# Another order of loads and blocks in the opening of a fused window attention and MLP kernel

## The chip, the cores and the metric

The kernel runs on one core of a Trainium2 chip. The metric is the device time of one execution in microseconds; the kernel before has a median of 288.01 us over three runs (287.84 to 289.57).

## The reference

Sliding-window attention, whose output feeds a two-layer MLP with a sigmoid-approximated gelu. Eight sequences of 576 tokens, 8 heads of 64; a token sees the 32 tokens on either side of it in its own sequence.

```python
scores = scale * np.matmul(q, k.transpose(0, 1, 3, 2))
mask = np.abs(pos[:, None] - pos[None, :]) <= 32
scores = np.where(mask, scores, -1000000000.0)
attn = np.exp(scores - max); attn = attn / sum
x = np.matmul(attn, v)                   # 4608 tokens x 512
h = x @ w_in                             # 512 -> 2048
g = h * (1.0 / (1.0 + np.exp(-1.702 * h)))
out = g @ w_out                          # 2048 -> 512, float32
```

## The kernel before, in words

The 4608 tokens are 36 units of 128 keys and 128 queries (the queries shifted by 32), four units to a tile of 512 tokens, nine tiles in all. A unit goes through these steps. `scores` (L238): 24 small matmuls into two PSUM banks (tag "t" is a pair of banks; "A", "C", "B", "E", "LA", "LB" are single ones), then two exponentials on ScalarE (L256) into `p`. `band` (L258): VectorE multiplies `p` by a 0/1 mask (L264). `values` (L266): 16 matmuls with `ve` (v as loaded) and `vo` (v shifted by 64 rows, built by `odd_v`, L201, from this unit's and the next unit's v), a column of ones giving the sums. `norm` (L284): VectorE divides. `x_T` and `x_T2` (L298, L313): TensorE transposes one unit's or two units' x, and VectorE or ScalarE copies it into `xT`.

A tile's layer 1 is `layer1_plain` for tile 0 (L378): sixteen blocks of 8 matmuls, each block followed by a gelu on ScalarE. From tile 1 on it is `l1_group` (L407): four groups of seven products by Strassen's scheme, which need sums of w_in (`w1_sums`, L327, in `a`) and of x (`x_sums`, L349, in `xs`), both made by VectorE. Layer 2 of tile 0 is plain (`layer2_plain`, L464): 64 matmuls of 512 columns, taken one by one from the list `l2` wherever the order has room for them; those of later tiles are Strassen's again (`layer2`, L492). Exponential and gelu need different tables on ScalarE, and each change of kind is a table load.

The order of every engine is written out by hand: an engine takes its instructions in the order in which the program names them and waits at each until its inputs and its buffer are there. Nothing is planned at run time. `opening` (L562) names everything up to the first product of tile 1; `run` (L785) then calls `x_sums(1)` and `first_layer1` (L845), whose four groups take 8 matmuls of `l2` each, and after it the scores of tile 2 and whatever is left in `l2`. All loads of inputs are issued by GpSimd, in the order of the program, so a load stands behind GpSimd's copies and mask work; each load of GpSimd also waits for the eighth load before it. The first 576 keys and queries are loaded in an order of their own (`load_first`, L137: two parts, each over 64 partitions) and transposed by TensorE (`T_first`, L157); the second tile's come with `load_four` and `T_four` (L173, L181). `keep_busy` (L553) issues filler matmuls on a tile of zeros, which TensorE runs while it has nothing else.

In the opening before, units 0 and 1 go through attention first, then the second half of k and q is transposed, four layer 1 blocks run between units 2 and 3, then twelve blocks between the transposes and attention of units 4 to 7, with 24 of the 64 matmuls of `l2`.

## Time and profile before

| | |
|---|---|
| runs | 287.84, 288.01, 289.57 us |
| profiled execution | 289.7 us, span of its instructions 288.0 us |
| TensorE busy | 277.7 us (96%) |
| VectorE, ScalarE, GpSimd busy | 218.3, 193.9, 126.9 us |
| chain that ended last | TensorE 87%, VectorE 4%, ScalarE 3% |
| read from HBM, written | 36.83 MB, 9.44 MB |

A row of the timeline has the start in us from the span's start, the time that the merged instructions took, the engine, the line of the program, the operation, output and inputs, shapes and the count; in brackets the idle time of the engine before it and what ended it. PE is TensorE's matmul, PEld its loading of weights, DVE is VectorE, ACT ScalarE, POOL GpSimd. Rows of helper lines (L67, L70) are told apart by their tiles: `sc` scores, `pv` values, `tp` transposes, `h` layer 1, `o` layer 2, `junk` filler. A row of a transfer has its count, size and the time from issue to landing.

### The profile page before, as it was taken

To read this page: it belongs to the slowest core of one execution; us is meant where nothing else is said; L and a number is where in the kernel's file an instruction comes from. 1 tells how busy PE (TensorE), PEld (TensorE's weight loads), DVE (VectorE), ACT (ScalarE), POOL (GpSimd) and SP (SyncE) were. 2 spreads that over 40 slices of the span, in tenths; PEclk is the share of its full clock that TensorE was granted. 3 is DMA by queue.
4 is the path that set the end of the run, shared out by engine and by line. 5 is a ranking of instruction groups with operands and counts; after the bars stand their busy time and mean duration, and the time that the engine had idled before them with its cause. 6 is when DMAs were issued, how large, how long until landed. Compare 5 with 4: busy or idle time off the path is not lost.

```text
span 288.0 us, 9119 instructions
## 1 busy us (share of the span) xinstructions
PE 277.7 (96%) x3770; PEld 229.8 (80%) x3770; DVE 218.3 (76%) x502; ACT 193.9 (67%) x340; POOL 126.9 (44%) x192
## 2 busy tenths in 40 slices
PE   7997999999999998999999999999999999999994
PEld 5775856777678887888888888888888888888883
DVE  0676798888877986798879887978788878946731
ACT  2437594789887668676967696689668865568410
POOL 8965457599499954467155917350210000000000
PEclk9999999999999999999999999999999999999999
DMA  8999999999999999999979999998432150301033
GB/s 94 188 193 198 184 204 153 177 99 140 184 134 153 209 132 198 93 180 146 182 106 181 142 177 100 193 116 148 95 77 64 47 112 12 81 2 73 2 110 112
DMA packets 146986, 37.37 MB, mean 130 GB/s; under 512 B 133888, under 2 KB 142592, under 8 KB 146944
## 3 DMA queue, kind: packets, MB, share of 16 engines
q0 software_dynamic: 104464, 18.42, 91.4%
q1 hardware_dynamic: 42032, 17.84, 34.8%
q8 instruction: 29, 0.48, 0.7%
q10 hardware_dynamic: 448, 0.52, 0.6%
q14 instruction: 13, 0.11, 0.1%
HBM read 36.83 MB, written 9.44 MB: 161 GB/s over the span
## 4 chain that ended last, share of the span: by engine, by line
PE 87%; DVE 4%; ACT 3%; issue 2%; DMA 2%; ACTq 0%; POOLq 0%
PE h L70 39%; PE o L70 36%; PE pv L70 3%; PE sc L70 3%; DVE x L294 2%; DMA kq<-in_k_dram 2%; PE junk L70 2%; ACT p L256 1%; PE tp L168 1%; PE tp L322 1%; ACT L256 1%; DVE p L264 1%; PE tp L189 1%; PE tp L232 1%; DVE rec L293 1%
## 5 line engine op out<-in xcount | busy, mean ns | idle before, releaser
L419 ACT ACTIVATE g<-h 128x512 f16<-128x512 f32 x128 | 72.1, 598 | 35.9 <-PE h L70 35.7
L70 PEld LDWEIGHTS <-g 128*128 128x128 f16 x576 | 54.5, 98 | 9.7
L70 PEld LDWEIGHTS <-a 128*128 128x128 f16 x512 | 49.3, 98 | 11.0 <-issue 0.8
L70 PE MATMUL h<-xs,a 128*128 128x256 f16 x384 | 57.6, 272 | 0.1
L70 PE MATMUL o<-w,g 128*128 128x256 f16 (+1 forms) x320 | 55.1, 294 | 0.0
L70 PEld LDWEIGHTS <-w 128*128 128x128 f16 x512 | 49.2, 98 | 7.3 <-issue 0.6
L70 PE MATMUL h<-xT,w 128*128 128x256 f16 x384 | 53.9, 273 | 0.6 <-issue 0.5
L199 POOL DMA_DIRECT2D ve<-in_v_dram x40 | 34.3, 863 | 44.0 <-issue 37.0
L70 PEld LDWEIGHTS <-gs 128*128 128x128 f16 x384 | 36.9, 98 | 6.2 <-issue 1.5
L256 ACT ACTIVATE p<-sc 128x512 bf16<-128x512 f32 x72 | 36.6, 619 | 3.7 <-PE sc L70 3.6
L70 PE MATMUL o<-b,gs 128*128 128x256 f16 x256 | 37.8, 273 | 1.3 <-issue 0.9
L70 PE MATMUL o<-b,g 128*128 128x256 f16 x256 | 37.3, 273 | 0.0
L432 DVE TENSOR_TENSOR h<-h,s 128x512 f32<-128x512 f32 x32 | 22.4, 698 | 18.7 <-PE h L70 18.7
L67 ACT COPY h<-h 128x512 f32<-128x512 f32 x32 | 18.7, 585 | 16.5 <-PE h L70 16.1
L131 POOL DMA_DIRECT2D kst<-in_k_dram x31 | 26.4, 855 | 6.9 <-PE tp L232 3.4
L131 POOL DMA_DIRECT2D qst<-in_q_dram x35 | 28.1, 805 | 2.8 <-DMA w<-in_moe_w_out_dram 2.7
L294 DVE TENSOR_TENSOR x<-pv,rec 128x256 f16<-128x256 f32 (+1 forms) x53 | 27.6, 520 | 1.8
L264 DVE TENSOR_TENSOR p<-p,mask 128x1024 bf16<-128x1024 bf16 x36 | 24.7, 687 | 2.6 <-ACT p L256 2.6
L438 DVE TENSOR_TENSOR h<-h,s 128x512 f32<-128x512 f32 x32 | 22.4, 700 | 4.7 <-PE h L70 4.2
L209 POOL COPY vo<-ve 64x264 int32<-64x264 int32 x28 | 13.1, 467 | 25.8 <-PE pv L70 24.7
L67 ACT COPY s<-h 128x512 f32<-128x512 f32 x32 | 19.1, 598 | 1.5 <-PE h L70 0.2
L70 PE MATMUL h<-xs,w 128*128 128x256 f16 x128 | 19.2, 273 | 0.0
(85 smaller groups left out, 367.9 us busy)
## 6 DMA issues: line engine op xcount, KB each, us to landing
out_dram<-o_sb SPq DMA_DIRECT2D x33, 256.0 KB, 3.0
ve<-in_v_dram POOLq DMA_DIRECT2D x32, 128.0 KB, 5.8
kst<-in_k_dram POOLq DMA_DIRECT2D x25, 128.0 KB, 5.9
qst<-in_q_dram POOLq DMA_DIRECT2D x21, 128.0 KB, 5.7
w<-in_moe_w_in_dram POOLq DMA_DIRECT2D x4, 512.0 KB, 8.7
w<-in_moe_w_out_dram POOLq DMA_DIRECT2D x4, 512.0 KB, 13.5
qst<-in_q_dram POOLq DMA_DIRECT2D x7, 96.0 KB, 5.1
kq<-in_q_dram POOLq DMA_DIRECT2D x2, 256.0 KB, 6.2
```

What stands on the lines that cost most here:

```text
L67: (eng.copy if eng is self.nc.scalar else eng.tensor_copy)(out, in_)
L70: self.nc.tensor.matmul(out, lhsT, rhs, start=start, stop=stop, skip_group_check=True)
L131: self.nc.gpsimd.dma_start(t[off:off + n], src[b, :, s:s + n, :].rearrange("h s d -> s h d"))
L168: self.nc.tensor.transpose(tp[64 * (h % 2):64 * (h % 2) + 64, h // 2, x, :], src[:, 4 * i + h, x, :], self.ident[r, r])
L199: self.nc.gpsimd.dma_start(t[off:off + n, :, :self.D], self.v[b, :, s:s + n, :].rearrange("h s d -> s h d"))
L209: eng.tensor_copy(words(vo[64:128]), words(self.ve[u % 9][64:128]))
L256: self.nc.scalar.activation(p[:, eo].rearrange("k h s -> k (h s)"), sc[eo], AF.Exp, scale=self.scale)
L264: (eng or self.nc.vector).tensor_mul(pv, pv, msk.to_broadcast([128, 8, 2, SQ]))
L294: dve.tensor_mul(x[:, 4 * at:4 * (at + n), :].rearrange("p (b h) d -> p b h d", b=n), acc[:, :, :, :D], r.to_broadcast([128, n, 4, D]))
L419: act.activation(g[:, f, 256 * half:256 * half + 256], bank.rearrange("p (i n) -> p i n", i=2), AF.Gelu_apprx_sigmoid)
L432: dve.tensor_add(e, b, s7)
L438: dve.tensor_add(c, b, s7)
```

## The change

- The first halves of k and q come in two loads each, over all 128 partitions, and are transposed with 128 columns instead of 64. v of units 0 to 3 and half of unit 4's are loaded ahead of w_in, the rest of unit 4's behind it; loads of v go ahead of w_out's.
- A matrix `far` (0 inside the window, -8e9 outside) is built by GpSimd. For units 0 to 3 and 5 to 7, TensorE adds it to the scores by two matmuls of 512 columns with the identity ahead of the scores; these units have no `band`. The 0/1 mask for the other units is made from `far` by VectorE, later.
- Units 0 to 3 go through attention ahead of layer 1. The sixteen blocks of tile 0 run in the order of w_in's quarters. The scores of units 4 to 7 are issued together, each in its own pair of banks.
- The opening takes 8 matmuls of `l2`, each group of `first_layer1` 14. All sums of w_in's second half stand at the end of the opening, ahead of `x_sums(1)`. The `odd_v` copies of units 3, 4 and 6 go to GpSimd. Fillers have half the width.

```diff
--- before.py
+++ after.py
@@ -96,19 +97,25 @@
         self.idle = cst.tile([128, 512], BF16, name="idle")
         self.spark = cst.tile([128, 1], F32, name="spark")
 
+    def setup_far(self):
+
+        pool, m = self.nc.gpsimd, self.far
+        lo, hi = slice(0, 64), slice(64, 128)
+        pool.memset(m, 0.0)
+        for b, rows, sign in ((0, lo, 1), (0, hi, -1), (1, lo, -1), (1, hi, 1)):
+            ap = m[rows, b, :]
+            pool.affine_select(out=ap, in_=ap, compare_op=ALU.is_ge, fill=-8.0e9, base=0,
+                               pattern=[[-sign, SQ]], channel_multiplier=sign)
+
     def setup_mask(self):
-        pool, m = self.nc.gpsimd, self.mask
+
+        dve, m = self.nc.vector, self.mask
         lo, hi = slice(0, 64), slice(64, 128)
-        pool.memset(m, 1.0)
-        for blks, rows, sign in ((slice(0, 2), lo, 1), (slice(0, 2), hi, -1), (slice(2, 4), lo, -1), (slice(2, 4), hi, 1)):
-            ap = m[rows, blks, :]
-            pool.affine_select(out=ap, in_=ap, compare_op=ALU.is_ge, fill=0.0, base=0,
-                               pattern=[[0, 2], [-sign, SQ]], channel_multiplier=sign)
-
-    def cut_mask(self):
-        lo, hi = slice(0, 64), slice(64, 128)
+        for b in range(2):
+            dve.tensor_scalar(out=m[:, 2 * b:2 * b + 2, :], in0=self.far[:, b:b + 1, :].to_broadcast([128, 2, SQ]),
+                              scalar1=0.0, scalar2=None, op0=ALU.is_ge)
         for b, rows, cols in ((0, hi, slice(0, 32)), (0, lo, slice(32, 64)), (2, lo, slice(0, 32)), (2, hi, slice(32, 64))):
-            self.nc.gpsimd.memset(self.mask[rows, b, cols], 0.0)
+            dve.memset(m[rows, b, cols], 0.0)
 
     def load_w1(self, c, n=1):
         w = 512 * n
@@ -135,13 +142,21 @@
     FIRST = {"k": ((0, 320, 5), (320, 256, 4)), "q": ((32, 256, 4), (288, 256, 4))}
 
     def load_first(self, c, part):
+
+        D = self.D
         if "first" not in self.stage:
-            s = self.sb("g", [128, self.H, 9, self.D], BF16, 2, "kq1")
-            self.stage["first"] = {"k": s[:, :, 0:5], "q": s[:, :, 5:9]}
+            s = self.sb("g", [128, 68 * D], BF16, 2, "kq1")
+            self.stage["first"] = {("k", 0): s[:, 0:20 * D], ("q", 0): s[:, 20 * D:36 * D],
+                                   ("k", 1): s[0:64, 36 * D:68 * D], ("q", 1): s[64:128, 36 * D:68 * D]}
         lo, n, j = self.FIRST[c][part]
-        src = {"q": self.q, "k": self.k}[c]
-        self.nc.gpsimd.dma_start(self.stage["first"][c][64 * part:64 * part + 64, :, 0:j],
-                                 src[0, :, lo:lo + n, :].rearrange("h (p j) d -> p h j d", j=j))
+        src = {"q": self.q, "k": self.k}[c][0, :, lo:lo + n, :].rearrange("h (p j) d -> p h (j d)", j=j)
+        dst = self.stage["first"][c, part]
+        if part:
+            self.nc.gpsimd.dma_start(dst.rearrange("p (h x) -> p h x", h=8), src)
+            return
+        for g in range(2):
+            self.nc.gpsimd.dma_start(dst[64 * g:64 * g + 64].rearrange("p (h x) -> p h x", h=4),
+                                     src[:, 4 * g:4 * g + 4, :])
 
     def kq_tile(self, t):
 
...
@@ -159,16 +174,24 @@  (T_first, the first half's new form)
+            tp = self.bank(tag, [128, j, 2, 64], BF16, "tp")
+            for x in range(j):
+                for h in range(2):
+                    self.nc.tensor.transpose(tp[64 * h:64 * h + 64, x].rearrange("x g p -> x (g p)"), src[:, 2 * i + h, x, :],
+                                             self.ident)
+            self.copy(eng, dst[:, i:i + 3:2, :].rearrange("x g (p j) -> x g p j", j=j), tp.rearrange("x j g p -> x g p j"))
...
@@ -198,6 +221,13 @@
         for off, b, s, n in self.pieces(128 * u, 128):
             self.nc.gpsimd.dma_start(t[off:off + n, :, :self.D], self.v[b, :, s:s + n, :].rearrange("h s d -> s h d"))
 
+    def load_v_part(self, lo, n):
+        u, at = divmod(lo, 128)
+        t = self.ve[u % 9]
+        for off, b, s, m in self.pieces(lo, n):
+            self.nc.gpsimd.dma_start(t[at + off:at + off + m, :, :self.D],
+                                     self.v[b, :, s:s + m, :].rearrange("h s d -> s h d"))
+
     def odd_v(self, u, eng):
 
         vo = self.vo[u % 5]
@@ -235,7 +265,7 @@
 
 
 
-    def scores(self, u, tag):
+    def scores(self, u, tag, far=False):
         kT, q = self.kT[u], self.qT[u]
         nxt = self.k_first if u == self.NU - 1 else self.kT[u + 1][:, :, 0:64]
         if tag == "t":
@@ -243,13 +273,17 @@
             sc = [sc[:, 0], sc[:, 1]]
         else:
             sc = [self.bank(x, name="sc") for x in tag]
+        if far:
+            m = self.far.rearrange("p (o b) s -> p o b s", o=1).to_broadcast([128, 4, 2, SQ])
+            for eo in range(2):
+                self.mm(sc[eo].rearrange("p (o b s) -> p o b s", b=2, s=SQ), self.ident, m, start=True)
         for hp in range(4):
             c = 128 * hp
             for eo in range(2):
                 r = slice(64 * eo, 64 * eo + 64)
                 lo, hi = sc[eo][0:64], sc[eo][64:128]
-                self.mm(lo[:, c:c + 64], kT[r, hp, 0:64], q[r, hp, 0:64], start=(hp == 0))
-                self.mm(hi[:, c:c + 128], kT[r, hp, 64:128], q[r, hp, :], start=(hp == 0))
+                self.mm(lo[:, c:c + 64], kT[r, hp, 0:64], q[r, hp, 0:64], start=(hp == 0 and not far))
+                self.mm(hi[:, c:c + 128], kT[r, hp, 64:128], q[r, hp, :], start=(hp == 0 and not far))
                 self.mm(lo[:, c + 64:c + 128], nxt[r, hp, :], q[r, hp, 64:128], start=False)
         p = self.p[u] = self.sb("p", [128, 2, 8, SQ], BF16, 4)
         for eo in range(2):
@@ -569,128 +603,109 @@
             dve.memset(t[:, :, self.D:], 1.0)
         self.load_first("k", 0)
         self.load_first("q", 0)
+        self.load_v(0)
         make_identity(nc, self.ident)
         act.activation(self.spark, self.spark, AF.Exp)
-        for u in (0, 1, 2):
-            self.load_v(u)
+        self.load_v(1)
+        self.load_first("k", 1)
+        self.setup_far()
+        self.load_first("q", 1)
+        self.load_v(2)
+        self.load_v(3)
+        self.load_v_part(512, 64)
         self.load_w1(0)
-        self.setup_mask()
-        self.load_first("k", 1)
-        self.load_first("q", 1)
-        self.cut_mask()
         self.load_w1(1)
-        self.load_v(3)
-        self.load_v(4)
+        self.odd_v(3, pool)
         self.load_w1(2)
         self.load_four("k")
         self.load_four("q")
         self.load_w1(3)
+        self.load_v_part(576, 64)
+        for u in (5, 6, 7, 8):
+            self.load_v(u)
+        for c in range(4):
+            self.load_w2(c)
         dve.tensor_copy(self.identh, self.ident)
-        self.keep_busy(20, "E")
+        self.keep_busy(44, "E", 128)
         self.T_first("k", 0, "AC", (dve, act))
-        self.keep_busy(6, "E")
+        self.keep_busy(4, "E", 128)
         self.T_first("q", 0, ("LA", "LB"), (dve, act))
-        self.keep_busy(4, "E")
-        for u in (5, 6):
-            self.load_v(u)
-        self.load_w2(0)
-        for u in (7, 8):
-            self.load_v(u)
-        for c in (1, 2, 3):
-            self.load_w2(c)
-        self.load_kq("k", 8)
-        self.scores(0, "t")
-        self.scores(1, "AC")
+        self.scores(0, "t", True)
+        self.scores(1, "AC", True)
         self.odd_v(0, dve)
+        self.keep_busy(6, "E", 128)
+        self.values(0, "t")
+        self.norm(0)
+        self.T_first("k", 1, ("LA", "LB"), (act, act))
+        self.keep_busy(8, "E", 128)
+        self.T_first("q", 1, "BE", (dve, act))
         self.odd_v(1, dve)
-        self.keep_busy(10, "E")
-        self.band(0)
-        self.band(1)
-        self.values(0, "t")
+        self.odd_v(2, dve)
+        self.keep_busy(10, "t", 128)
+        self.scores(2, "t", True)
+        self.scores(3, ("LA", "LB"), True)
         self.values(1, "AC")
-        self.norm(0)
         self.norm(1)
-        self.keep_busy(6, "E")
-        self.x_T(0, "LA", act)
-        self.keep_busy(4, "E")
-        self.x_T(1, "LB", act)
-        self.T_first("k", 1, "AC", (dve, dve))
-        h, n, gelus = [], [0], []
+        self.keep_busy(4, "B", 128)
+        self.values(2, "t")
+        self.norm(2)
+        self.x_T2(0, "A", act)
+        self.values(3, ("LA", "LB"))
+        self.norm(3)
+        self.x_T(2, "E", act)
+        h, n = ["C", "B", "LA", "LB", "C", "B", "A", "E", "LA", "LB", "B", "E"], [0]
 
         def l1(half, *ds):
             for d in ds:
-                self.layer1_plain(0, d, half, h[n[0] % len(h)])
+                self.layer1_plain(0, d, half, h[n[0]])
                 n[0] += 1
 
-        self.layer1_plain(0, 0, 0, "B", gelus)
-        self.T_first("q", 1, ("LA", "LB"), (dve, act))
-        self.layer1_plain(0, 1, 0, "E", gelus)
-        self.odd_v(2, dve)
-        self.odd_v(3, dve)
-        h[:] = ["LB", "B", "E"]
-        self.scores(2, "t")
-        self.scores(3, "AC")
-        self.layer1_plain(0, 2, 0, "LA", gelus)
-        self.layer1_plain(0, 3, 0, "LB", gelus)
-        self.do(gelus)
-        self.band(2)
-        self.band(3)
-        self.values(2, "t")
-        self.norm(2)
-        self.values(3, "AC")
-        self.norm(3)
-        self.x_T2(2, "A", dve)
-        l1(0, 4)
+        l1(0, 0)
+        l1(0, 1)
+        self.x_T(3, "A", dve)
+        l1(1, 0, 1)
+        self.setup_mask()
         dve.tensor_copy(self.k_first, self.kT[0][:, :, 0:64])
         dve.tensor_copy(self.v_first, self.ve[0][0:64])
+        for i in (3, 1, 2, 4):
+            self.w1_sums((i,), 0)
+        self.odd_v(4, pool)
+        self.odd_v(6, pool)
+        self.load_kq("k", 8)
         for u in (8, 9, 10, 11):
             self.fetch(u)
-        l1(1, 0, 1)
+        l1(0, 2, 3)
+        l1(1, 2, 3)
+        l1(0, 4, 5)
         halo = self.kT[4]
-        self.T_four("k", "AC", (dve, dve))
+        self.T_four("k", "AC", (dve, act))
         dve.tensor_copy(self.kT[4][:, :, 0:64], halo)
-        l1(1, 2, 3)
-        l1(0, 5)
-        self.T_four("q", "AC", (dve, act))
         l1(1, 4, 5)
-        self.odd_v(4, dve)
+        self.T_four("q", ("LA", "LB"), (dve, act))
         self.scores(4, "t")
-        self.scores(5, "AC")
-        for i in (3, 1, 2, 4):
-            self.w1_sums((i,), 0)
+        self.scores(5, "AC", True)
+        self.scores(6, "BE", True)
+        self.scores(7, ("LA", "LB"), True)
         self.odd_v(5, dve)
-        for d, tag in ((6, "B"), (7, "E")):
-            self.layer1_plain(0, d, 0, tag, gelus)
-        self.do(self.l2, 3)
-        self.scores(6, "t")
-        self.do(self.l2, 3)
-        self.scores(7, "AC")
-        self.do(gelus)
-        self.do(self.l2, 2)
         self.band(4)
-        self.band(5)
-        self.odd_v(6, dve)
         self.odd_v(7, dve)
-        self.band(6)
         self.values(4, "t")
         self.norm(4)
-        self.band(7)
         self.values(5, "AC")
         self.norm(5)
+        self.values(6, "BE")
+        self.norm(6)
+        self.values(7, ("LA", "LB"))
+        self.norm(7)
+        self.x_T2(4, "t", act)
+        self.layer1_plain(0, 6, 0, "A")
+        self.layer1_plain(0, 7, 0, "C")
+        self.layer1_plain(0, 6, 1, "B")
+        self.layer1_plain(0, 7, 1, "E")
+        self.x_T2(6, "t", dve)
+        for i in (3, 1, 2, 4):
+            self.w1_sums((i,), 1)
         self.do(self.l2, 8)
-        self.values(6, "t")
-        self.norm(6)
-        self.values(7, "AC")
-        self.norm(7)
-        h[:] = "BE"
-        n[0] = 0
-        for i in (3, 1):
-            self.w1_sums((i,), 1)
-        l1(1, 6, 7)
-        self.x_T2(4, "A", act)
-        self.do(self.l2, 4)
-        self.x_T2(6, "t", dve)
-        self.do(self.l2, 4)
 
     def fetch(self, u):
         self.load_kq("q", u)
@@ -844,7 +859,7 @@
 
     def first_layer1(self):
 
-        dv = [lambda i=i: self.w1_sums((i,), 1) for i in (2, 4)]
+        dv = []
         for n in range(4):
             if n == 3:
                 self.turn(12)
@@ -853,7 +868,7 @@
             self.fetch(12 + n)
 
             def fill(i):
-                self.do(self.l2, {1: 1, 7: 1, 2: 3, 4: 3}[i])
+                self.do(self.l2, {1: 2, 7: 2, 2: 5, 4: 5}[i])
                 self.do(dv, {1: 2, 7: 1, 2: 0, 4: 2}[i] if n else 0)
                 if i == 7 and n:
                     self.T_pe([("k8", "q8", "k9"), ("q9", "k10", "q10"), ("k11", "q11", "k12")][n - 1], self.nc.scalar)
```

21 lines of the change are left out of this document (12 added, 9 removed).

## The prediction

> **What bounds the kernel now.** I read the page first (span, engines, chain), then the timeline of the first 55 us, in which the changed part lies, then the timeline of 70 to 78 us, where the leftover of layer 2 is used up today, and last the transfers of the first 60 us.
>
> ```profile
> span 288.0 us, 9119 instructions
> PE 277.7 (96%) x3770; PEld 229.8 (80%) x3770; DVE 218.3 (76%) x502; ACT 193.9 (67%) x340; POOL 126.9 (44%) x192
> PE 87%; DVE 4%; ACT 3%; issue 2%; DMA 2%; ACTq 0%; POOLq 0%
> ```
>
> TensorE is busy throughout and holds 87% of the chain. From 50 us on its order is full of real products, so a microsecond won or lost on TensorE before that moves the end by the same amount. In the opening TensorE is "busy" in another sense: it runs filler matmuls and waits for neighbours.
>
> ```profile
> L70 PE MATMUL junk<-idle 128*128 128x256 bf16 x50 | 10.5, 384 | 1.3 <-DVE spark L567 1.3
> 1.27 4.45 PE L70 MATMUL junk<-idle 128*128 128x256 bf16 x20 [1.27 <-DVE spark L567]
> 6.34 1.35 PE L168 MATMUL tp<-ident,kq 64*64 64x64 bf16 x40 [0.63 <-DMA kq<-in_k_dram]
> 12.01 2.08 PE L70 MATMUL junk<-idle 128*128 128x256 bf16 x10
> 14.94 0.83 PE L70 MATMUL junk<-idle 128*128 128x256 bf16 x6
> 17.59 0.60 PE L70 MATMUL h<-xT,w 128*128 128x256 f16 x4
> 35.53 0.59 PEld L70 LDWEIGHTS <-kq 64*64 64x64 bf16 x48 [0.21 <-issue]
> 49.46 0.60 PE L70 MATMUL h<-xT,w 128*128 128x256 f16 x4
> ```
>
> These are the marks of the opening: first transposes at 6.34 when k lands, first product of layer 1 at 17.59, twelve of the sixteen layer 1 blocks and all transposes of the second load done at 35.53 (scores of unit 4), first product of tile 1 at 49.46. Ten of the first 17 us are filler.
>
> ```profile
> 26.16 2.78 PE L70 MATMUL h<-xT,w 128*128 128x256 f16 x24
> 28.88 1.11 PE L189 MATMUL tp<-ident,o_sb 128*64 128x128 bf16 x32
> 41.88 1.90 PE L70 MATMUL o<-w,g 128*128 128x512 f16 x8
> 49.90 0.38 PE L70 MATMUL o<-w,g 128*128 128x512 f16 x1
> 37.55 4.03 ACT L256 ACTIVATE p<-sc 128x512 bf16<-128x512 f32 x8
> 10.21 0.59 ACT L67 COPY kq<-tp 128x512 bf16<-128x512 bf16 x1 [1.79 <-PE tp L168]
> 47.54 1.01 ACT L67 COPY xT<-tp 128x1024 f16<-128x1024 f16 x1
> 38.74 0.69 DVE L264 TENSOR_TENSOR p<-p,mask 128x1024 bf16<-128x1024 bf16 x1
> ```
>
> These are the prices. A layer 1 block is 8 matmuls; 24 span 2.78 us with about 0.2 us of pipeline at the end, so one block is 0.88 us. A layer 2 matmul of 512 columns is (1.90 - 0.38) / 7 = 0.217 us. A transpose of 128 columns in the paired form takes about 0.03 us. ScalarE copies 512 columns in 0.59 us and 1024 in 1.01. One exponential costs ScalarE 4.03 / 8 = 0.50 us, a band 0.69 us of VectorE.
>
> **The change part by part.** First, work that is added and removed. Seven units get two mask matmuls of 512 columns each: 14 x 0.217 = 3.0 us of TensorE at full speed. The trace has no matmul with a broadcast operand; the layer 2 row is the nearest in columns, the other bound is nothing (all of it inside waits). Units 0 to 3 have four of the seven, issued while TensorE would wait for the evacuation of q; I count those of units 5 to 7, 1.3 us, on the path. Seven bands leave VectorE, 7 x 0.69 = 4.8 us, and each was a link between exponential and values. ```profile
> GB/s 0 6 110 195 170 154 199 213 186 199 208 169 181 212 193 196 192 200 207 185 170 203 189 174 205 206 205 203 192 156 148 160 147 155 158 147 121 288 158 110
> 1.33 0.82 POOL L143 DMA_DIRECT2D kq<-in_k_dram  x1 [0.80 <-POOLq L896]
> 2.14 0.69 POOL L143 DMA_DIRECT2D kq<-in_q_dram  x1
> 7.18 1.34 POOL L105 TENSOR_SCALAR_AFFINE_SELECT mask<-mask 64x128 bf16<-64x128 bf16 x4
> 9.02 1.09 PE L168 MATMUL tp<-ident,kq 64*64 64x64 bf16 x32
> kq<-in_k_dram POOLq DMA_DIRECT2D x1, 320.0 KB, 5.0
> ```
>
> The k and q rows are GpSimd's issues, 0.82 and 0.69 us; each is now two issues of half the size, 0.4 to 0.8 us each, so the last is out up to 1 us later. Today q is used at 9.02, behind a filler; the issue at 2.14 is followed by a landing that I put at 7.8 (k: 1.33 + 5.0 = 6.33, q 256 KB behind it at 0.17 MB per us), and at 8.2 in the change (7.8 to 8.8). Building `far` costs GpSimd about what the mask's four selections do today, 1.34 us, ahead of q's second half; it delays nothing that TensorE waits for, unless it ends after 8.8 us.
>
> Second, the loads. Each column of the rate is 1.5 us: 1.25 MB have moved by 10.5 us, 1.85 MB by 13.5, and the queue is never dry after 4 us. In the new order the second halves of k and q stand behind two units of v, 1.38 MB in all, so q lands near 12.3, unit 3 of v and half of unit 4 (1.70 MB) near 14, the first quarter of w_in (2.23 MB) near 17. GpSimd's copy `odd_v(3)` waits there until 14, but the two quarters of w_in queued before it, 1.05 MB, last 5 us, so the queue stays full. The order of the loads gives all it promises; what follows is set by hand-overs.
>
> Third, the hand-overs to the first layer 1 block. q at 8.2, 16 transposes to 8.8, evacuations to 9.7, scores 0, four exponentials 10.3 to 12.3. ScalarE then evacuates k's second half (two copies, 0.59 each) to 13.5, q's follows to 14.4, scores 2 and 3 to 15.8, their exponentials to 17.3; the values of unit 1 follow scores 3, and VectorE divides them until about 17.6, x of units 0 and 1 is transposed to 18.0 and copied by ScalarE (1.0 us) to 19.1. Layer 1 starts at 19.2 instead of 17.59, with units 2 and 3 nearly through.
>
> Fourth, the middle. Twelve blocks (10.6), x of unit 3 with the wait for its copy (0.2 + 0.8), both sets of 32 transposes (1.9) and 0.5 us for the changes of group: 33.2 instead of 35.5. Then nothing stands between the transposes and scores 4: the last copy of q (1.0 us after 0.3) leaves TensorE idle for 1.3, scores 4 run at 34.5. ScalarE reloads its table (1.28) and does eight exponentials, 34.5 + 1.3 + 8 x 0.5 = 39.8; values 7 end at 40.2. Two transposes of x (1.0), four blocks (3.5) and eight layer 2 matmuls (1.7) follow: 46.4. I take 46.0 (44.5 to 48), since the groups overlap a little at their ends: tile 1 starts 3.5 us earlier.
>
> But layer 2 of tile 0 has done 8 of 64 matmuls there, not 24. **This is the heart of the sum.** The other 56 go into the four groups of tile 1, 14 in each instead of 8. TensorE is the bound of those groups, so 24 x 0.217 = 5.2 us come back at once.
>
> ```profile
> 46.63 1.28 DVE L335 TENSOR_TENSOR a<-w 128x1024 f16<-128x1024 f16 x2
> 48.80 0.69 DVE L67 COPY xT<-tp 128x1024 f16<-128x1024 f16 x1 [0.88 <-PE tp L322]
> 49.53 0.85 DVE L354 TENSOR_TENSOR xs<-xT 128x512 f16<-128x512 f16 x2
> 50.12 0.60 PE L70 MATMUL h<-xs,a 128*128 128x256 f16 x4
> 54.27 1.28 DVE L67 COPY o_sb<-o 128x512 f32<-128x512 f32 x2
> 65.85 0.68 DVE L346 TENSOR_TENSOR b<-w,b 128x1024 f16<-128x1024 f16 x1
> 53.06 0.70 DVE L438 TENSOR_TENSOR h<-h,s 128x512 f32<-128x512 f32 x1 [0.16 <-PE h L70]
> ```
>
> Two new waits follow. (a) Today two sums of w_in (1.28) run before the copy of x's last pair, and the sums of x start right behind it, 49.53. In the change all four sums of the second half stand between: copy, 4 x 0.65, then the first sum of x, 0.43. Product 7 of the first group needs that one, 0.27 + 0.69 + 2.6 + 0.43 + 0.05 = 4.0 us after the last transpose, while TensorE has 8 + 2 layer 2 matmuls and product 1, 2.6 us: 1.4 us idle. (b) The first half of layer 2 now ends inside group 1, in the fill behind product 4. Its second bank is evacuated on VectorE behind the addition (0.70) and a w_out sum (0.68): about 0.27 + 0.7 + 0.68 + 0.64 = 2.3 us after product 5, while product 4 and three layer 2 matmuls give 1.1; the next one needs that bank: 1.1 us idle (0 to 1.2).
>
> ```profile
> 70.19 1.68 ACT L419 ACTIVATE g<-h 128x512 f16<-128x512 f32 x3 [0.33 <-PE h L70]
> 71.80 1.90 PE L70 MATMUL o<-w,g 128*128 128x512 f16 x8
> 71.89 1.28 ACT L256 ACT_TABLE_LOAD   x1
> 73.19 2.06 ACT L256 ACTIVATE p<-sc 128x512 bf16<-128x512 f32 x4
> 75.11 0.62 ACT L67 COPY o_sb<-o 128x512 f32<-128x512 f32 x1
> 76.55 0.45 ACT L67 COPY o<-o 128x256 f32<-128x256 f32 x1
> 76.85 0.44 ACT L67 COPY s7o<-o 128x256 f32<-128x256 f32 x1
> 77.05 1.03 PE L70 MATMUL o<-b,gs 128*128 128x256 f16 x8 [0.46 <-ACT o L67]
> ```
>
> (c) Behind tile 1's groups a chain on ScalarE sets the pace: gelus to 71.87, table, exponentials, copies, and TensorE's product 6 waits for it at 77.05. Today eight layer 2 matmuls (1.7 us) lie under that chain for nothing. The change has none left for it, so their 1.7 us, paid above, are not given back; the o copy (0.5) leaves the chain but now stands ahead of the last gelus and delays them by about as much.
>
> The sum, against the profiled execution's 288.0: -3.5 (opening) + 5.2 (24 matmuls) + 1.4 (a) + 1.1 (b) + 0 (c) = +4.2 us, so product 6 starts near 81.2 instead of 77.05, with the same work done on both sides. Behind it nothing differs. The execution with the span 288.0 took 289.7 in all; the runs' median is 288.01, so I carry the difference to the median: **292.2 us**.
>
> **The clock.** Twenty fillers in a row take 4.45 us, 0.21 each; so do the ten at 12.01; the six at 14.94 take 0.83, 0.11 each. TensorE therefore ran at half speed until about 13.7, though the page prints a full clock. The change has 44 fillers of half the width, 4.7 us in a row at that speed instead of 4.3, and afterwards mostly transposes, masks and short fillers. I take full speed from 6 to 10 us; if it stays half until 13, scores, masks and fillers on the path above take 1.7 us more.
> The Trainium skill (TensorE: Matmul & The Clock Gate, Part 1) puts the rise after some 3.4 us of sustained activity in a free-running window, and says in its transpose section that transposes do not count as busy. Here 4.3 us of fillers were not enough, which agrees only if the window fell badly; by the rule with a good window, 44 fillers give full speed near 6 and the sum stays as it is, with a bad one it is 1.7 more.
>
> **The rivals.** 1. *The opening hands over without gaps* (not slower). If copies and exponentials hide, TensorE after w_in's first quarter (17.1) has 16 blocks (14.1), transposes (2.8), scores, masks and values (3.0), 8 layer 2 matmuls (1.7) and 1 us of changes left: 39.7. With 41 instead of 46.0 the sum is 287.2. It decides if the first block starts by 17.5 and scores 4 wait under 0.3. For it: the bands are gone from VectorE. Against it: eight exponentials and a table load in a row, 5.3 us, with only some 3 us of scores, masks and values beside them. 2. *VectorE is not late in tile 1*: if (a) and (b) vanish, 289.7. Against it: the order of VectorE's work is written out, and the rows above leave no slack. 3. *Half clock and late landings* (slower than forecast): half speed to 13 (+1.7) and q half a microsecond later (+0.5), 294.4. 4. *The masks cost more than columns*: with none of units 0 to 3 hidden, 4 x 2 x 0.217 = 1.7 more, 293.9.
>
> **How the numbers follow.** Forecast with its neighbours (291 to 293.5): 0.45. Rival 3 with 4 (above 293.5): 0.15. Rival 2 and part gains in the opening (288.5 to 291): 0.22. Rival 1 (285 to 288.5): 0.12. Something I do not see, below 285: 0.06. One per cent is 2.9 us, about what a measurement can tell; 290.9 parts "slower" from "within". Slower by over 1%: the first two, 0.45 + 0.15, and 0.02 of the third, 0.62. Within 1%: the rest of the third and rival 1, 0.32. Faster: 0.06. The range 287.0 to 295.3 leaves about a tenth on each side.
>
> **What would show it.** Right: layer 1 begins near 19, scores 4 near 34.5 behind an idle stretch, tile 1 near 46, an idle TensorE ahead of its first product with xs, another behind the middle of group 1, and product 6 near 81. Wrong: layer 1 before 17.5, tile 1 before 43, or no idle time at those places. A row of fillers at 0.11 us per 256 columns before 8 us shows the early clock.

## The result: slower, and the profile after

The changed kernel takes 297.35 us (median of four runs, 296.62 to 298.27) against 288.59 for the kernel before on the same chip: 1.029 times as long, with a 95% interval of 1.0255 to 1.0324. The forecast was 292.2 with a range up to 295.3. The sign was right, the size was not. Here and below, ratios and intervals leave out executions over 1.5% slower than their kernel's fastest, three in all, while medians hold every execution. Both profiled executions, 298.27 us here and 289.7 before, lie about 1 us above their medians.

The page of the changed kernel: span, busy times, the chain's shares.

```profile
span 296.5 us, 9128 instructions
PE 278.6 (94%) x3774; PEld 231.0 (78%) x3774; DVE 209.9 (71%) x494; ACT 196.8 (66%) x343; POOL 129.4 (44%) x196
PE 84%; DVE 6%; ACT 3%; issue 2%; POOL 2%; DMA 2%; POOLq 0%; DVEq 0%
```

TensorE is busy for 0.9 us more than before, in a span that is 8.5 us longer: 7.6 us of the loss are idle time. VectorE's load fell by 8.4 us, and its share of the chain still rose, 4% to 6%. The table of waits of the changed kernel's TensorE up to 50 us (total, number of times, longest) says for what it stood still; these are three of its rows. "Issue" is a wait with nothing behind it that the profile can name.

```profile
PE tp L192 <- DMA kq<-in_q_dram: 1.3, 1, 1.3
PE pv L70 <- issue: 1.3, 1, 1.3
PE tp L184 <- issue: 0.8, 1, 0.8
```

The timeline of the changed kernel's TensorE, at the marks that the prediction set:

```profile
8.40 0.64 PE L192 MATMUL tp<-ident,kq 128*64 128x128 bf16 x16 [1.30 <-DMA kq<-in_q_dram]
13.28 0.59 PE L184 MATMUL tp<-ident,kq 64*64 64x64 bf16 x24 [0.21 <-DMA kq<-in_q_dram]
14.66 0.32 PE L184 MATMUL tp<-ident,kq 64*64 64x64 bf16 x8 [0.79 <-issue]
21.05 0.19 PE L70 MATMUL pv<-vo,p 128*64 128x65 bf16 x1 [1.30 <-issue]
21.61 3.36 PE L70 MATMUL h<-xT,w 128*128 128x256 f16 x16
37.67 0.55 PE L70 MATMUL sc<-kq 64*64 64x64 bf16 x24 [0.87 <-DVE kq L67]
50.16 0.60 PE L70 MATMUL h<-xT,w 128*128 128x256 f16 x4
52.38 0.61 PE L70 MATMUL h<-xs,a 128*128 128x256 f16 x4 [1.18 <-DVE xs L388]
64.54 0.59 PE L70 MATMUL o<-w,g 128*128 128x512 f16 x2 [0.90 <-DVE o_sb L67]
84.92 1.03 PE L70 MATMUL o<-b,gs 128*128 128x256 f16 x8
```

| mark, us from the span's start | before | forecast | after |
|---|---|---|---|
| first layer 1 block | 17.59 | 19.2 | 21.61 |
| scores of unit 4 | 35.53 | 34.5 | 37.67 |
| first product of tile 1 | 49.46 | 46.0 | 50.16 |
| product 6 behind tile 1's groups | 77.05 | 81.2 | 84.92 |
| end of the span | 288.0 | 292.2 | 296.5 |

From tile 1's start to product 6 the kernels need 84.92 - 50.16 = 34.76 and 77.05 - 49.46 = 27.59 us, so the change costs 7.2 us; the forecast had 7.7. Behind product 6 they need 211.6 and 211.0 us, 0.6 more. So what is missing lies in the opening, ahead of 50 us: the forecast won 3.5 us there and the kernel lost 0.7, 4.2 us apart.

Two things in it were in no step of the sum. In the middle of rows of transposes and of values, TensorE stops twice with nothing to wait for, 0.79 and 1.30 us. And the first two blocks of layer 1 take 3.36 us for 16 matmuls, where 0.88 us a block were counted. The windows view of the changed kernel shows the second as half clock; after the stretch's limits and length come PE, PEld, DVE, ACT and POOL busy with their counts, then the granted clock, the DMA share and GB/s:

```profile
17.80:21.20 3.40, 2.09 (x54) 1.47 (x49) 2.44 (x8) 2.00 (x4) 3.40 (x5) 0.99 1.22 198
21.20:24.60 3.40, 3.40 (x22) 2.55 (x20) 0.61 (x2) 2.47 (x3) 1.83 (x3) 0.50 1.35 190
```

A stretch of 3.4 us in which TensorE was busy for 2.09 us, with the standstill in it, is followed by one at half clock, just when the first products of layer 1 run; from 24.6 us on the clock is full again.

### The profile page after: what moved, and what is told of

It is laid out like the page before. It is cut to its first block, busy times and chain, and to the rows that moved or that the text cites. A ratio compares the mean times of both kernels' runs of the same rounds, so it can differ in the third digit from the quotient of the medians.

```text
span 296.5 us, 9128 instructions
## 1 busy us (share of the span) xinstructions
PE 278.6 (94%) x3774; PEld 231.0 (78%) x3774; DVE 209.9 (71%) x494; ACT 196.8 (66%) x343; POOL 129.4 (44%) x196
## 3 DMA queue, kind: packets, MB, share of 16 engines
q1 hardware_dynamic: 42032, 17.84, 34.8%
## 4 chain that ended last, share of the span: by engine, by line
PE 84%; DVE 6%; ACT 3%; issue 2%; POOL 2%; DMA 2%; POOLq 0%; DVEq 0%
PE h L70 38%; PE o L70 35%; PE sc L70 4%; PE pv L70 4%; DMA kq<-in_q_dram 2%; ACT p L290 1%; DVE x L328 1%; PE tp L356 1%; POOL kq L158 1%; PE tp L262 1%; DVE xs L388 1%; DVE a L369 1%; DVE p L298 1%; DVE xT L67 1%; POOL ve L222 1%
## 5 line engine op out<-in xcount | busy, mean ns | idle before, releaser
L70 PEld LDWEIGHTS <-w 128*128 128x128 f16 x512 | 50.2, 99 | 7.7 <-DVE xT L67 0.7
L70 PE MATMUL o<-w,g 128*128 128x256 f16 (+1 forms) x320 | 54.3, 294 | 0.9 <-DVE o_sb L67 0.9
L70 PE MATMUL h<-xT,w 128*128 128x256 f16 x384 | 54.5, 278 | 0.5 <-DVE xT L67 0.5
L222 POOL DMA_DIRECT2D ve<-in_v_dram x38 | 32.8, 866 | 44.4 <-issue 36.1
L466 DVE TENSOR_TENSOR h<-h,s 128x512 f32<-128x512 f32 x32 | 22.4, 699 | 21.2 <-PE h L70 21.2
L67 ACT COPY h<-h 128x512 f32<-128x512 f32 x32 | 18.7, 585 | 16.5 <-PE h L70 14.4
L239 POOL COPY vo<-ve 64x264 int32<-64x264 int32 x31 | 14.1, 454 | 31.4 <-PE pv L70 28.0
L298 DVE TENSOR_TENSOR p<-p,mask 128x1024 bf16<-128x1024 bf16 x29 | 19.9, 685 | 4.2 <-ACT p L290 4.2
L70 PE MATMUL h<-xs,w 128*128 128x256 f16 x128 | 19.2, 273 | 0.0
```

Of the source, the lines that this page charges most:

```text
L67: (eng.copy if eng is self.nc.scalar else eng.tensor_copy)(out, in_)
L70: self.nc.tensor.matmul(out, lhsT, rhs, start=start, stop=stop, skip_group_check=True)
L222: self.nc.gpsimd.dma_start(t[off:off + n, :, :self.D], self.v[b, :, s:s + n, :].rearrange("h s d -> s h d"))
L239: eng.tensor_copy(words(vo[64:128]), words(self.ve[u % 9][64:128]))
L298: (eng or self.nc.vector).tensor_mul(pv, pv, msk.to_broadcast([128, 8, 2, SQ]))
L466: dve.tensor_add(e, b, s7)
```

## The experiments

My theory of the standstills: TensorE waits for its own instructions. Among the transfers there are packets of 16 KB on a queue of kind "instruction". Each trace has 29 of them, and TensorE has 7586 instructions in the changed kernel, 29.6 times 256, loads of weights and waits on semaphores counted. Every wait of TensorE for "issue" of 0.4 us or more, in the traces of all twelve kernels of this document, ends at one of the same few instruction numbers, counted that way from 0: 449, 705, 2497, 3265 and, within two, 4033. They are whole multiples of 256 apart. From the start of the block's last instruction to the start of the next they last 0.98 us (449) and 1.49 us (705) in the changed kernel and 0.75 us (705) in the kernel before; the rows' own idle time is shorter, since a matmul's end is counted as busy. I read such a packet as the next block, since one follows each entry of TensorE into a block of 256. In the openings of the two kernels it comes 0.9 to 4.4 us after the entry, and at the standstills of all openings the first instruction of the new block runs 2.2 to 2.6 us after the packet starts. A block that TensorE gets through faster than the two together ends in a standstill. For 705 of the changed kernel: block entered at 14.66, packet at 18.66, work done at 19.6, next instruction at 21.05. The first rival: the stops are hidden waits for banks or engines, and stay with the place in the program. The second: the loss is the hand-overs alone. The third: the half clock has a cause of its own. The other open points were the price of the moved layer 2 matmuls, waits (a) and (b), and the masks.

**Half as many fillers, of twice the width.** The same filler time in 22 matmuls instead of 44 moves each block's end 44 instructions further on in the work.

```diff
-        self.keep_busy(44, "E", 128)
+        self.keep_busy(22, "E", 256)
```

> The changed kernel with its first 44 fillers of 128 columns written as 22 of 256: the same columns, 44 TensorE instructions fewer. Theory (instruction supply): TensorE stands still wherever it reaches the end of a block of 256 instructions sooner than about 2.4 us after the load of the next block starts; both standstills of the opening (0.8 us at 14.66, inside the second half of q's transposes, and 1.4 us at 21.05, at the last value matmul of unit 3) move 44 instructions later in the program, the first into fillers, the second into layer 1, where they are hidden. No window is then empty enough to lose the clock near 21. Expected: layer 1 starts near 20, no half clock there, 3 to 4.5 us less, about 293.5. Rival (fetch position does not matter; the standstills come from transfers or hand-overs): the standstills stay at the same instructions and the time stays at 297.4 within 0.7. Rival (half clock has its own cause, the many short matmuls): the standstills move, the clock still drops near 21, and only 1 to 2 us are won.

294.5 us, 1.0199 (1.016 to 1.0237), 2.85 less than the changed kernel and a little short of the 3 to 4.5 that I expected. Timeline of this kernel's TensorE, and its windows:

```profile
13.54 0.71 PE L184 MATMUL tp<-ident,kq 64*64 64x64 bf16 x32 [0.90 <-DMA kq<-in_q_dram]
19.77 1.91 PE L70 MATMUL h<-xT,w 128*128 128x256 f16 x16
46.88 0.60 PE L70 MATMUL h<-xT,w 128*128 128x256 f16 x4
81.64 1.03 PE L70 MATMUL o<-b,gs 128*128 128x256 f16 x8
```

```profile
17.80:21.20 3.40, 3.06 (x52) 2.36 (x45) 2.33 (x8) 2.73 (x4) 3.40 (x6) 1.00 1.20 189
21.20:24.60 3.40, 2.88 (x29) 2.46 (x27) 1.86 (x10) 2.25 (x5) 1.70 (x3) 1.00 1.36 198
```

The 32 transposes run in one row, the first block starts 1.84 us earlier, and its 16 matmuls take 1.91 us instead of 3.36: 1.45 more. Together that is the 3.28 us between 50.16 and 46.88. The attention and layer 1 work is the same; only the count of instructions ahead of it differs. Neither 449 nor 705 has a standstill now. That speaks for the theory and against the first two rivals. It does not settle the third: two of its six executions still have a mean granted clock of 0.993 or 0.994, and one stretch of 3.4 us at half clock in a span of 296 us makes 0.994. Product 6 starts at 81.64, 0.4 us from the forecast, and the span is 292.5.

**The layer 2 shares as before.**

```diff
-                self.do(self.l2, {1: 2, 7: 2, 2: 5, 4: 5}[i])
+                self.do(self.l2, {1: 1, 7: 1, 2: 3, 4: 3}[i])
```

> The changed kernel with tile 1's groups taking 8 layer 2 matmuls each, as before, instead of 14; 24 are then left and run behind the scores of units 8 and 9. Theory (part c of the sum: layer 2 of tile 0 is worth its place under the exponentials of tile 2): tile 1's groups get 5.2 us shorter, the standstill behind the middle of group 1 (0.9) goes, and of the 5.2 us of layer 2 behind the scores some 2 to 2.5 lie under the chain on ScalarE: 2 to 3.5 us less, about 294.5. Rival (the same TensorE work in another place costs the same): within 0.9 us of 297.4, which is the standstill alone.

295.55 us, 1.023 (1.0181 to 1.0279). Its TensorE's timeline:

```profile
14.32 0.72 PE L184 MATMUL tp<-ident,kq 64*64 64x64 bf16 x32 [1.38 <-DMA kq<-in_q_dram]
20.77 0.19 PE L70 MATMUL pv<-vo,p 128*64 128x65 bf16 x1 [0.97 <-issue]
21.16 1.91 PE L70 MATMUL h<-xT,w 128*128 128x256 f16 x16
48.27 0.60 PE L70 MATMUL h<-xT,w 128*128 128x256 f16 x4
70.53 0.60 PE L70 MATMUL h<-xs,a 128*128 128x256 f16 x4 [1.06 <-DVE h L466]
73.21 5.35 PE L70 MATMUL o<-w,g 128*128 128x512 f16 x24
81.39 1.05 PE L70 MATMUL o<-b,gs 128*128 128x256 f16 x8
```

The 24 matmuls now run as one row of 5.35 us behind the groups, 0.22 each. Their cost of 5.2 us in the forecast is right, but not all of it is lost there: tile 1's start to product 6 takes 33.1 us instead of 34.8. Some of the row lies under ScalarE's chain, wait (b) is gone, and a new wait of 1.06 us for VectorE's addition (70.53) takes part back. The gain of 1.8 us is a little under the 2 to 3.5 expected, and the interval overlaps the changed kernel's, so it rests on the trace.
Up to tile 1 this is the program of the changed kernel, executed once more. It has the standstill at 705 (1.16 us from start to start), none at 449, where the second half of q came later, and a full clock from 6.8 us on; tile 1 starts 1.9 us earlier than in the changed kernel's profile. So the changed kernel's loss in the opening differs between executions, and a standstill at 705 is not always followed by half clock.

**The sums of w_in ahead of the last x.**

```diff
-        self.x_T2(6, "t", dve)
         for i in (3, 1, 2, 4):
             self.w1_sums((i,), 1)
+        self.x_T2(6, "t", dve)
```

> The changed kernel with the four sums of w_in's second half put ahead of the transposes of x of units 6 and 7, where VectorE is idle for 2.3 us. Theory (part a): the sums of x follow the copy at once, the standstill of 1.2 us ahead of the first product with xs shrinks to 0 to 0.4, and 0.8 to 1.2 us are won, about 296.4. Rival (the standstill covers something else that is late, such as the copies of ScalarE): no change within 0.4.

296.23 us, 1.0251 (1.0213 to 1.0288). Its TensorE's timeline:

```profile
49.86 0.60 PE L70 MATMUL h<-xT,w 128*128 128x256 f16 x4
50.73 0.60 PE L70 MATMUL h<-xs,a 128*128 128x256 f16 x4
83.26 1.03 PE L70 MATMUL o<-b,gs 128*128 128x256 f16 x8
```

Product 7 follows 0.87 us after the first product instead of 2.22. Tile 1's start to product 6 shrinks by 1.36 us: wait (a) was the sums in VectorE's order. The median is 1.1 us under the changed kernel's, as expected, but the intervals overlap, and this execution ran at half clock from 13.8 to 20.6 us; the trace is the better evidence.

**All three together.**

> The changed kernel with all three edits: 22 fillers of 256 columns, 8 layer 2 matmuls in each group of tile 1, the four sums ahead of the last transposes of x. Theory: the gains lie at different places and add up, less the clock's part that differs between executions: 2.9 + 1.6 to 2.5 + 1.2 = 5.7 to 6.6 us less than the changed kernel's 297.4, about 291.2; without standstills the opening ends near 46.9, and what is left against the kernel before is that the opening did 16 layer 2 matmuls (3.5 us) less for a start of tile 1 that is only 2.5 us earlier, and the rest of the 24 matmuls that does not fit under the exponentials. Rival (the gains overlap: each edit only moves the wait to the next place): 292.5 to 294.

292.19 us, 1.0114 (1.0073 to 1.0155). Its TensorE's timeline:

```profile
46.89 0.60 PE L70 MATMUL h<-xT,w 128*128 128x256 f16 x4
47.54 0.60 PE L70 MATMUL h<-xs,a 128*128 128x256 f16 x4
77.96 1.05 PE L70 MATMUL o<-b,gs 128*128 128x256 f16 x8
86.98 0.60 PE L70 MATMUL h<-xT,w 128*128 128x256 f16 x4 [1.35 <-issue]
```

The three gains were 2.85, 1.80 and 1.12 us, 5.8 in all; together they give 5.2, between the theory's time and the rival's. Against the kernel before, measured beside each of them, the three edits take 0.9, 0.6 and 0.4 points off the ratio of 1.029, and together 1.8, so they nearly add up. Product 6 is 0.9 us later than before. An idle time of 1.35 us stands at 86.98, at a block's end (instruction 2497), behind a row of scores, and no standstill is there in the changed kernel: the stops move with the count.

**The kernel before with 40 narrow fillers** instead of 20 wide ones, so that the block that ends at 705 ends in the scores of unit 3, where instructions are shortest.

```diff
-        self.keep_busy(20, "E")
+        self.keep_busy(40, "E", 128)
```

> The kernel before with its first 20 fillers of 256 columns written as 40 of 128: the same columns, 40 TensorE instructions more. Theory (instruction supply): the end of the third block moves 40 instructions earlier, from layer 1 block 3 into the scores of unit 3 or the blocks right ahead of it, so the 0.75 us standstill at 22.7 comes earlier in the program, ahead of exponentials that wait for these scores, and costs 0.3 to 1.2 us: 288.5 to 290. Rival (position does not matter): the standstill stays in front of the same matmul of layer 1 and the time is the same within 0.3.

288.12 us, 0.9985 (0.9958 to 1.0012). Its TensorE's timeline:

```profile
19.86 0.28 PE L70 MATMUL sc<-kq 64*64 64x128 bf16 x8 [1.14 <-issue]
48.01 0.60 PE L70 MATMUL h<-xT,w 128*128 128x256 f16 x4
```

The stop went where the count put it, into the last eight matmuls of unit 3's scores, and no bank or engine had changed there. The rival's place is refuted. The time did not follow: it is 0.4 us below the range that the theory gave, and the ratio's interval holds 1. In this execution the clock was full from 6.5 us instead of 13.7, which may hide the cost; that is not shown.

**The clock early in the kernel before,** by four more fillers.

```diff
-        self.keep_busy(20, "E")
+        self.keep_busy(24, "E")
```

> The kernel before with 24 fillers at the start instead of 20; the four more lie in the time in which TensorE waits for k. Theory (the clock rises after a window with at least some 70% of matmul time): 5.1 us of fillers in a row hold such a window in nearly every execution, the clock is full from 5 to 7 us on instead of 13.7, and the opening ends up to 1.5 us earlier: 287.2, between 286.5 and 288.2. Rival (the opening is bound by landings and hand-overs and the clock there costs nothing): 288.6 within 0.4.

288.92 us, 1.0003 (0.9982 to 1.0023): no gain. Its TensorE's timeline, and behind it two rows of the kernel before:

```profile
21.72 1.03 PE L70 MATMUL h<-xT,w 128*128 128x256 f16 x8 [1.52 <-issue]
24.73 0.83 PE L322 MATMUL tp<-identh,x 128*128 128x128 f16 x8 [1.34 <-DVE x L294]
49.11 0.60 PE L70 MATMUL h<-xT,w 128*128 128x256 f16 x4
```

```profile
22.77 0.60 PE L70 MATMUL h<-xT,w 128*128 128x256 f16 x4 [0.47 <-issue]
25.35 0.83 PE L322 MATMUL tp<-identh,x 128*128 128x128 f16 x8 [1.35 <-DVE x L294]
```

The clock was full from 4.3 us and the first block came at 15.88, 1.7 us earlier. The stop at 705 grew from 0.75 to 1.79 us from start to start and took about 1.0 of it back. The wait for VectorE behind it is as long as before (1.34 and 1.35) and comes 0.6 us earlier; tile 1 starts 0.35 earlier. The rival's time was met: in this kernel the early clock brings no measurable gain.

**Wider fillers against the loss of the clock.**

```diff
-        self.keep_busy(8, "E", 128)
+        self.keep_busy(8, "E", 256)
...
-        self.keep_busy(4, "B", 128)
+        self.keep_busy(4, "B", 512)
```

> The changed kernel with wider fillers at two places where TensorE waits anyway: eight of 256 columns instead of 128 ahead of the second half of q, four of 512 instead of 128 ahead of the values of unit 2. The number and order of instructions is the same. Theory (the clock falls to half where a window of 3.4 us holds under about a quarter of matmul time, transposes not counted): both standstills stay at the same instructions, the two thin windows (0.23 to 0.29 in the traces so far) rise to 0.35 or more, the clock stays full from the first rise on, and 0.5 to 1.5 us are won (1.5 from the clock, up to 0.7 lost to the fillers): about 296.4. Rival (the clock falls for another reason): the clock still falls somewhere between 10 and 25 us and the time is 297.4 to 298.

296.39 us, 1.027 (1.0232 to 1.0308): the expected number, though the interval overlaps the changed kernel's. The windows of the profiled execution:

```profile
11.70:15.20 3.50, 2.13 (x64) 1.63 (x60) 1.75 (x4) 1.37 (x3) 1.18 (x2) 0.99 1.89 154
15.20:22.00 6.80, 6.38 (x89) 3.58 (x90) 2.10 (x8) 2.76 (x5) 5.96 (x9) 0.50 1.23 197
```

Here the clock fell in another place, and for two stretches: at 15.1 instead of 21.2 us, ahead of the second edit. But this is the exception: at 299.26 us and a mean clock of 0.989 it is the slowest of six, and the other five have 0.998 to 1.000 and take 295.72 to 297.23 us. With the changed kernel's opening (the changed kernel itself and the runs with the layer 2 shares and the sums edited) 12 of 16 executions are below 0.995. So the wider fillers mostly kept the clock, as the theory says. It is not proved: the executions are few, on different chips, and in the profiled one the stretch of 11.7 to 15.2 us was thin in spite of the first edit.

**The masks alone, in the kernel before.** Seven units get their mask from TensorE, their bands go, the order stays (two of the places).

```diff
-        self.scores(0, "t")
-        self.scores(1, "AC")
+        self.scores(0, "t", True)
+        self.scores(1, "AC", True)
...
-        self.band(0)
-        self.band(1)
```

> The kernel before with the masks alone: units 0 to 3 and 5 to 7 get their mask by two matmuls of 512 columns on TensorE, their bands on VectorE go, the 0/1 mask for the other units is made later by VectorE; order, loads and layer 2 stay as before. Theory (the prediction's term, masks of units 5 to 7 on the path and the others half hidden): 3.0 us of matmuls come in, 1 to 2 of them on TensorE's path, and the bands' going wins 0.7 to 1.5 back in front of the values of units 0 to 3: 289, between 288.2 and 290. Rival (the masks themselves are what makes the changed kernel slow): 291 or more. Rival (bands were the wait of the opening): 286.5 to 287.5.

288.98 us, 1.0000 (0.9975 to 1.0026). In that order the masks cost nothing net and win nothing, to within 0.3%; cost and gain are not told apart.

**The instruction load given a free queue.** GpSimd's copy for unit 3, which waits for v, moves ahead of the first two loads of w_in, so that the transfers run dry at 15 us.

```diff
+        self.odd_v(3, pool)
         self.load_w1(0)
         self.load_w1(1)
-        self.odd_v(3, pool)
```

> The changed kernel with GpSimd's copy of unit 3's v put ahead of the first two quarters of w_in instead of behind them. GpSimd waits for v of units 3 and 4 there, so the transfer queue runs dry for 1 to 3 us near 14 to 17 us; instructions and fillers stay the same. Theory (the load of the next 256 TensorE instructions starts when TensorE enters a block, but stands behind the loads of inputs for 2 to 4 us before its 2.4 us): the load that today starts at 18.7 for the end of the block at 21.08 starts near 15 to 16, the standstill of 1.4 us there goes, and the thin window with it; w_in's first quarter lands near 19 instead of 17, in time for layer 1 near 20: 1.4 to 3 us less than 297.4, about 295. The first standstill at 14.7 stays. Rival (the load of instructions has a lead of its own and does not depend on the traffic): the standstill stays, and the later w_in costs 0 to 1 us: 297.4 to 298.5.

297.12 us, 1.0278 (1.0244 to 1.0312). The view of the transfers, changed kernel first: 14.7 to 18.6 us, nearly all of the 4.0 us after TensorE's entry into the block at 14.66, then 18.6 to 19.0. A line has the queue and its kind, then packets, MB, and the time that they took as a share of 16 engines' span.

```profile
q0 software_dynamic: 809, 0.78, 123.8%
```

```profile
q0 software_dynamic: 76, 0.08, 114.5%
q8 instruction: 1, 0.02, 14.6%
```

The same view of the kernel with the gap: 14.4 to 15.8 us, where the loads run out, and 15.8 to 16.3.

```profile
q0 software_dynamic: 148, 0.02, 20.4%
```

```profile
q8 instruction: 1, 0.02, 11.6%
```

In the changed kernel the transfer engines move only input data until the packet comes, at 18.66. With the gap TensorE enters that block at 14.28 and the packet comes at 15.88, after 1.6 us instead of 4.0, and the standstill at its end is gone. TensorE was slower in this block, partly at half clock; but 15.88 and 2.4 us are 18.3, ahead of the 19.6 at which the changed kernel was through, so at that pace too there would be none. This fits the theory, and the wait behind the input loads is the larger part of the 4.0 us. The time missed the theory's 295 and came near the rival's. In this execution the clock fell twice, as its windows show, but that does not explain the miss: three of the six executions have a mean clock of 1.000 and take 296.64 to 297.33 us. The last row below has the first block of layer 1 waiting for w_in and starting at 21.56, against 21.61 in the changed kernel: in this trace nothing of what the standstill set free is left there. How much of it the later w_in took is not told apart.

```profile
15.10:18.50 3.40, 3.34 (x59) 1.41 (x58) 0.68 (x2) 1.24 (x4) 3.25 (x6) 0.51 0.21 18
42.40:45.80 3.40, 3.40 (x34) 2.65 (x29) 2.68 (x11) 2.13 (x2) 2.37 (x3) 0.51 1.24 205
```

```profile
21.56 1.92 PE L70 MATMUL h<-xT,w 128*128 128x256 f16 x16 [0.27 <-DMA w<-in_moe_w_in_dram]
```

**The kernel before with all its fillers 512 wide,** about half as many (six lines like this one).

```diff
-        self.keep_busy(20, "E")
+        self.keep_busy(12, "E", 512)
```

> The kernel before with all fillers of its opening 512 columns wide and half as many, and 12 (24 of the old width) at the start: about 46 TensorE instructions fewer ahead of the third block's end. Theory (instruction supply): the standstill of 0.75 to 1.8 us, which falls into layer 1 ahead of units 2 and 3's values in the kernel before and with 24 fillers, moves behind the values of unit 2, where TensorE waits for VectorE anyway; with the early clock the opening ends 1 to 1.5 us earlier: 287.6 against 288.9. Rival (the waits for transfers and VectorE behind it take the gain back): 288.5 to 289.3, the same within 0.4.

288.76 us, 0.999 (0.9962 to 1.0018). The standstill that the kernel before has at 705 (0.75 us, 22.02 to 22.77) is gone, tile 1 starts at 49.46 as before, and the time is the rival's. Its windows:

```profile
20.30:23.70 3.40, 1.66 (x42) 1.14 (x40) 3.30 (x9) 3.37 (x7) 2.32 (x4) 1.00 1.34 201
23.70:27.10 3.40, 3.39 (x22) 2.36 (x20) 1.30 (x4) 1.15 (x3) 1.62 (x3) 0.52 1.45 196
```

This execution has a stretch at half clock behind it, and by their mean clocks (0.991 to 0.994) so have seven of the twelve, 288.60 to 290.42 us; the other five take 286.97 to 288.32. Of 17 executions of the kernel before, run beside it, six have a clock that low. No version is measurably faster than the kernel before.

## Why the prediction was wrong in size, point by point

**The step that failed is the opening: the third part (hand-overs) and the fourth (middle), the term of -3.5 us. It measured +0.7.** The missing 4.2 us divide by the rows above. The standstills and what they delay are 1.84 us, the half clock behind them 1.45; both are absent in the profile with 22 fillers, whose opening gives -2.6. Another execution of the same opening (the run with the layer 2 shares as before) had less of both, so this is the bill of the profiled execution. Neither the standstills nor a fall of the clock was in the sum. The remaining 0.9 are sizes, and with 22 fillers they lie behind scores 4: the first block came at 19.77 instead of 19.2 (q's second half was put at 12.3, and its transposes ran at 13.54 with an idle wait ahead), but scores 4 were at 34.39 against 34.5. From there the row of eight exponentials was to start 1.3 us later; in the changed kernel's ScalarE, below, it starts 39.61 - 37.67 = 1.94 after, because the table load waits for the scores and their 0.55 us were not counted. The other 0.4 is what the prediction took off its own 46.4 for overlap.

```profile
38.32 1.28 ACT L290 ACT_TABLE_LOAD   x1 [0.47 <-PE sc L70]
39.61 4.03 ACT L290 ACTIVATE p<-sc 128x512 bf16<-128x512 f32 x8
```

**Where the instruction wait could have been seen.** The kernel before has it too, 0.75 us at 705. The prediction used "the queue is never dry" as good news for the loads; by the run with the gap it is also why the packet was late. What the change altered and the prediction did not price was the count: 44 fillers for 20, transposes and scores closer together, so that the block up to 449, which took 7.3 us in the kernel before (9.79 to 17.05) and had no standstill, was through in 3.9 us (9.77 to 13.68).
The Trainium skill (Runtime: NRT & Kernel Launch, Instruction fetch mechanics) says that instructions come in blocks of 16 KiB, 256 instructions, over the sequencer's own queue, and that crossing a boundary is mostly hidden. The block's size agrees with the packets here; "mostly hidden" does not hold in this opening, where two of the changed kernel's crossings cost 0.98 and 1.49 us.

**The clock.** Full speed from 6 to 10 us erred on the safe side: it came at 4.1. That it could be lost again was in no case: rival 3 had the clock late, not falling. All four executions of the changed kernel have a mean granted clock of 0.988 to 0.994, the profiled one 0.994 with one such stretch in it, so none was free of it. Rival 3's price, 1.7 us, is near the 1.45 that the fall cost here.
The Trainium skill (TensorE: Matmul & The Clock Gate, Part 1) says that the window of 3.4 us is free-running and that the clock falls after an idle window. The 3.4 us lengths agree; here windows with 1.66 to 2.24 us of recorded work were followed by half clock, so a wholly idle one was not needed.

**What was right.** The 24 layer 2 matmuls in tile 1's groups: 0.22 each, 5.35 for 24 in a row, against 5.2. Wait (a): 1.18 against 1.4. Wait (b): 0.90 against 1.1, at the second half's first matmul (64.54). From the last product 3 to product 6, (c): 6.4 us before (70.64 to 77.05) and 6.5 after (78.46 to 84.92), so about 0. Taken together 7.2 against 7.7. The masks of units 5 to 7, counted at 1.3 us, are not told apart by a run: in the order of before they cost nothing net, which leaves rival 4 without support. Rival 1 fails (first block at 21.61, scores 4 wait 0.87), rival 2 fails (both waits are there), and rival 3 came nearest, for another reason.

**What stays open.** When exactly the clock falls: busy time does not decide it alone, since the profiled execution of the kernel before with 24 fillers kept its clock after a stretch of 3.4 us with 1.67 us of recorded work (21.2 to 24.6), and the kernel with 512-wide fillers lost it after 1.66. That the standstills make it fall is therefore not shown; the two went together in the changed kernel's profile and not in that of the run with the layer 2 shares. What the kernel with three edits still loses is not divided either: its ratio is 1.0114, while its profiled execution, its fastest, has a span only 1.2 us longer than that of the kernel before, 0.9 of it there at product 6. Its standstill at 2497 (1.42 us from start to start) stands against one of 1.14 us at 3265 in the kernel before (the row below), which it does not have:

```profile
111.63 0.94 PE L70 MATMUL o<-b,gs 128*128 128x256 f16 x7 [0.86 <-issue]
```

## What to carry to other kernels

Count TensorE's instructions, not only its microseconds: where small matmuls pass 256 instructions in a few microseconds while the transfer queue is full, the engine may stop for its own program, and half as many fillers of double width fill the same time. Work that is moved pays only if the place it goes to has idle time: here 24 matmuls left an opening that waits and went into groups where each took its full 0.22 us. When a profile says "issue" in the middle of a row of like instructions, look at the instruction packets early.

## What the runs showed of the hardware

Packets of 16 KB on a queue of kind "instruction" come once for each 256 instructions of TensorE, among the transfers of the inputs: 4.0 us after TensorE's entry into a block in the full stretch at 14.7 us of the changed kernel, 1.6 with the queue dry, and at the standstills of the openings 2.2 to 2.6 more until the first instruction of the next block runs. The granted clock fell after 3.4 us with 1.66 to 2.24 us of recorded TensorE work and stayed at half for 3.4 to 6.8 us; it fell at 15, 14, 21, 24 or 42 us in kernels that differ by a few fillers. An early full clock brought the kernel before no measurable gain: 288.92 us, a ratio of 1.0003 (0.9982 to 1.0023).
